# The entry to an FFN: where five transposed tiles are put, who evicts them, and in which order three accumulators are filled

## The chip, the cores and the metric

The kernel runs on one NeuronCore of a Trainium2 chip. The metric is the device time of one execution in microseconds. The kernel before was run three times: 1008.08, 1010.73 and 1012.32 us, median 1010.73.

Names of engines in the profile: PE is TensorE (matmuls and transposes), DVE is VectorE, ACT is ScalarE, POOL is GpSimd, SP is SyncE, which up to now issues all DMAs. PEld is TensorE's loading of weights.

## The reference

The kernel computes one block of a network over a sequence of L = 2048 positions of width D = 640: a layer norm with modulation, an S4D convolution over the sequence, a second layer norm with modulation, and a gated FFN of inner width 1728.

```python
mod = (_silu(c) @ w_mod).reshape(c.shape[0], 6, 1, -1)
sa, ca, ga, sb, cb, gb = ...
h = _layernorm(x) * (1 + ca) + sa
x = x + ga * S4D(h)                       # long convolution by FFT
h = _layernorm(x) * (1 + cb) + sb
gate = h @ w1                             # [2048, 640] @ [640, 1728]
up   = h @ w3
out  = (_silu(gate) * up) @ w2            # [2048, 1728] @ [1728, 640]
x = x + gb * out
```

All in float32. The change touches the second layer norm of the first quarter of the positions and the FFN's first tiles.

## The kernel before, in words

The first 390 us compute the S4D branch: tables, the kernel's spectrum, the transforms, their product, and the first half of the inverse transform, whose result goes to a DRAM tensor `zd`. Their order is laid down by a planner (`Plan`, with ranks written into the file), and all their instructions carry line 156.

What follows is in program order with priorities, and a scheduler of the tile framework orders each engine's instructions from it. The 2048 positions are worked on in four blocks b = 0 to 3 of 512 positions. `self.x2[b]` holds a block as 128 partitions x 4 groups j x 640, and KT = 5 counts the chunks k of 128 channels.

Entry to the FFN, block 0, in this order:

- `inverse_load` (L630) reads the last 128 channels of `zd` for block 0 into the two tiles `izb0` and `izb1`, in four DMAs of 128 KB, all on SP's queue. They wait for the last store to `zd` (`zd<-zt`). Behind them SP issues `load_x2(1)`, four loads of 320 KB into `x2[1]`, then four more for `x2[2]` and eight `iz` loads.
- `inverse` (L640) multiplies them by `wd` into tiles `iy` in PSUM (L647), and DVE adds these to `x2[0]` (L650).
- `ln2` (L661) takes the statistics (L341, L345, a reciprocal square root of 13 small DVE instructions, L320 to L332), normalises the four groups j (`xn`, two on ACT at L674, two on DVE at L672), and transposes `xn` chunk by chunk: for each k four 128x128 transposes into one PSUM bank `tp` (L680). Then DVE makes `v` from the bank (L682, scale and shift), ACT makes `xh`, the same value rounded to float32r, from the same bank (L683), and DVE, or POOL for odd k in block 0, makes the rest `xl = v - xh` (L684). So a float32 product is done as three float32r matmuls: `wh*xh + wh*xl + wl*xh`.
- `ffn` (L728) goes through 14 tiles m of the inner width, in the order 0, 13, 1, 2, ... 12. `up` (L747) fills accumulators `gu`: two (gate and up) for a full tile, one for the half tile 13, which holds both halves. Each takes 15 matmuls (5 chunks x 3; L753, L754, L755). `gate` (L759) makes `th` on ACT (L767), `a` on DVE (L768, L769), `ah` on ACT and `al` on DVE (`split`, L657 to L659); for tile 13 it takes `th` and `u` on ACT (L773, L775) and more on DVE. `down` (L783) multiplies `ah` and `al` by `w2` into the five accumulators `acc` (L788 to L790), one tile behind `up`.
- The weights of the next tiles are split into `wh` and `wl` on ACT (L658) and DVE (L659) as soon as the tile two before has been used up. Those of the first two tiles are ready before the entry.

PSUM has eight banks. In this stage five belong to the pool `po`, one for each `acc`, and three to the tag `gu` of the pool `ps`, shared by the accumulators `gu`, by the tiles `iy` of the inverse transform (its remaining units are worked in between the FFN tiles of block 0), by `tp`, and by the output's transposes `to`. A `gu` bank is free again once its readers are done: for tile 0's first accumulator that is L768, for its second L769, for tile 13's the instruction at L777.

Of the kernel before, what the change touches and what calls it, by code (L numbers as in the profile page):

```python
# [10 lines left out]
F32 = mybir.dt.float32  # L11
F32R = mybir.dt.float32r
I32 = mybir.dt.int32
AF = mybir.ActivationFunctionType
ALU = mybir.AluOpType
# [3 lines left out]
P = 128  # L19
L = 2048  # L20
D = 640
KT = D // P
# [255 lines left out]
class K:  # L278
# [348 lines left out]
            self.nc.sync.dma_start(self.x2[b][q * 32:(q + 1) * 32], self.xv[q, :, 4 * b:4 * b + 4, :])  # L627


    def inverse_load(self, name, pool, tag, bufs, j0, nj, d0, d1):  # L630

        zv = self.zd.rearrange("f r t d -> (f r) t d")
        z = [pool.tile([P, nj, d1 - d0], F32, name=f"{name}{pr}", tag=f"{tag}{pr}", bufs=bufs) for pr in range(2)]
        for pr in range(2):
            for g in range(2):
                t0 = 16 * (2 * pr + g) + j0
                self.zload = self.nc.sync.dma_start(z[pr][g * 64:(g + 1) * 64], zv[:, t0:t0 + nj, d0:d1])
        return z

    def inverse(self, j0, nj, z, ps, tag, bufs, d0, d1):  # L640
# [17 lines left out]
        self.nc.scalar.activation(H, v, AF.Copy)  # L658
        eng.tensor_tensor(Lo, v, H.bitcast(F32), op=ALU.subtract)  # L659

    def ln2(self, b, pool, ps, stats=None, tag="gu"):  # L661

        nc = self.nc
        xs = self.x2[b]
        st, mv = stats or self.ln_begin(pool, f"n{b}")
        for j in range(4):
            self.ln_part(st, xs, j, KT - 1 if stats else 0, KT)
        rstd, nb = self.ln_end(pool, st, mv, f"n{b}")
        xn = pool.tile([P, 4, D], F32, name=f"xn{b}", tag="xn", bufs=1)
        for j in range(4):  # L670
            if j % 2:
                nc.vector.tensor_scalar(xn[:, j, :], xs[:, j, :], rstd[:, j:j + 1], nb[:, j:j + 1], op0=ALU.mult, op1=ALU.add)  # L672
            else:
                nc.scalar.activation(xn[:, j, :], xs[:, j, :], AF.Identity, scale=rstd[:, j:j + 1], bias=nb[:, j:j + 1])  # L674
        xh = pool.tile([P, KT, 512], F32R, name=f"xh{b}", tag="xh", bufs=2)
        xl = pool.tile([P, KT, 512], F32R, name=f"xl{b}", tag="xl", bufs=2)
        for k in range(KT):
            pt = ps.tile([P, 512], F32, name=f"tp{b}{k}", tag=tag, bufs=4 if tag == "f" else 3)
            for j in range(4):
                nc.tensor.transpose(pt[:, j * P:(j + 1) * P], xn[:, j, k * P:(k + 1) * P], self.ident)  # L680
            v = pool.tile([P, 512], F32, name=f"v{b}{k}", tag="v", bufs=2)
            nc.vector.tensor_scalar(v, pt, self.cols[:, 1, k:k + 1], self.cols[:, 0, k:k + 1], op0=ALU.mult, op1=ALU.add)  # L682
            nc.scalar.activation(xh[:, k, :], pt, AF.Identity, scale=self.cols[:, 1, k:k + 1], bias=self.cols[:, 0, k:k + 1])  # L683
            (nc.gpsimd if b == 0 and k % 2 else nc.vector).tensor_tensor(xl[:, k, :], v, xh[:, k, :].bitcast(F32), op=ALU.subtract)  # L684
        return xh, xl

    def weights(self, b, m, wp):
# [40 lines left out]
    def ffn(self, nxt, wp, pool, ps, po, mid):  # L728

        pend = None  # L730
        for b in range(4):
            acc = [po.tile([P, 512], F32, name=f"acc{b}{k}", tag=f"acc{k}") for k in range(KT)]
            for i in range(14):
                m = self.ORDER[i]
                wh, wl, w2h, w2l = self.ahead.pop((b, i), None) or self.weights(b, m, wp)
                gu = self.up(b, m, wh, wl, *nxt[b], ps)
                if pend is not None:
                    self.down(*pend)
                    if i == 0:
                        self.output(b - 1, pend[1], pool, ps)  # L740
                ah, al = self.gate(b, m, gu, pool)
                pend = (m, acc, ah, al, w2h, w2l)
                mid(b, i)
        self.down(*pend)
        self.output(3, acc, pool, ps)

    def up(self, b, m, wh, wl, xh, xl, ps):  # L747
        nc = self.nc
        gu = []
        for i in range(2 if m < 13 else 1):  # L750
            pg = ps.tile([P, 512], F32, name=f"gu{b}_{m}{i}", tag="gu", bufs=3)
            for k in range(KT):
                nc.tensor.matmul(pg, wh[:, i, k, :], xh[:, k, :], start=(k == 0), stop=False)  # L753
                nc.tensor.matmul(pg, wh[:, i, k, :], xl[:, k, :], start=False, stop=False)  # L754
                nc.tensor.matmul(pg, wl[:, i, k, :], xh[:, k, :], start=False, stop=(k == KT - 1))  # L755
            gu.append(pg)
        return gu

    def gate(self, b, m, gu, pool):  # L759
# [53 lines left out]
    def run(self):  # L813
# [7 lines left out]
        def open_(name, side=None, bufs=1, space=None):  # L821
            scopes[name] = ExitStack()
            return self.pool(name, bufs=bufs, space=space, ctx=scopes[name], side=side)
# [19 lines left out]
        nc = self.nc = Engines(self, real)  # L843
# [16 lines left out]
        b = NB - 1  # L860
# [14 lines left out]
        cut = b * P  # L875
        z = {}
# [19 lines left out]
        xp, ip, wp = self.xp, self.ip, self.wp  # L896
        pool = open_("ffn", "right")
        close("psx", "psg")
        po = open_("po", space=PSUM)
        ps = open_("ps", space=PSUM)  # L900
        self.x2 += [pool.tile([P, 4, D], F32, name=f"x2{b}") for b in range(1, 4)]
        z = self.inverse_load("izb", ip, "izb", 1, 0, 4, cut, D)
        self.inverse(0, 4, z, ps, "gu", 3, cut, D)
        nxt = {0: self.ln2(0, pool, ps, self.stats)}
        self.at(2000)
        self.load_x2(1)

# [563 lines left out]
```

## Time and profile before

| | |
|---|---|
| median of 3 runs | 1010.73 us (1008.08 to 1012.32) |
| profiled execution | 1012.95 us, its span 1010.6 us |
| TensorE busy in the span | 891.2 us, 88% |
| VectorE, ScalarE, GpSimd busy | 656.8, 507.8, 279.4 us |
| mean granted TensorE clock | 0.962 |
| first FFN matmul of block 0 | 408.28 us after the span's start |

The span runs from the first to the last instruction; the execution's time holds 2.35 us around it. In the profile a matmul's record lasts longer than its distance to the next one, since matmuls are pipelined: the row says 0.39 us for one of 512 columns, but they follow each other every 0.23 us at full clock and every 0.43 us at half clock. A row of the chain of waits gives start, length, engine and tile, in the order of time; a row of the timeline adds in brackets how long the engine sat idle before it and what ended that.

### The profile page before, as it was taken

What the parts mean: (1) busy time and instruction counts of PE and PEld (TensorE: products, weight loads), DVE (VectorE), ACT (ScalarE), POOL (GpSimd) and SP (SyncE); (2) the same over time, 40 slices, a digit from 0 to 9 for tenths busy, and PEclk for the clock granted to TensorE, in tenths of its full rate; (3) what the DMA queues carried; (4) which work ended last, traced back from release to release, by engine and by line L of the source; (5) the groups of instructions that cost most, each with busy time, mean ns of one, the idle gap of its engine ahead of it and who ended that gap; (6) DMA issues with size and microseconds to landing.
All of it is one profiled execution on the core that took longest, in us unless ns stands there. A gap on an engine that the chain in (4) does not pass through costs nothing.

```text
span 1010.6 us, 20260 instructions
## 1 busy us (share of the span) xinstructions
PE 891.2 (88%) x8129; PEld 714.0 (71%) x8129; DVE 656.8 (65%) x1214; ACT 507.8 (50%) x843; POOL 279.4 (28%) x288
## 2 busy tenths in 40 slices
PE   1463878788999885999999999999999999999996
PEld 1132756767887773677788888888888888888884
DVE  6998999999999475677664453464543643634332
ACT  6878787989787541432243343343433432533231
POOL 1798798988998200100000000000000000000000
PEclk9887998999999897899999999999999999999998
DMA  9955553624131759976232363332534333533302
GB/s 214 266 183 174 120 135 95 152 65 107 44 86 51 192 137 229 232 176 164 86 94 76 107 157 91 94 101 66 138 110 117 83 86 93 146 102 92 103 14 53
DMA packets 140998, 122.05 MB, mean 121 GB/s; under 512 B 13416, under 2 KB 124776, under 8 KB 139368
## 3 DMA queue, kind: packets, MB, share of 16 engines
q1 hardware_dynamic: 140904, 120.75, 45.4%
q8 instruction: 64, 1.05, 0.4%
q14 instruction: 30, 0.25, 0.1%
HBM read 99.75 MB, written 20.97 MB: 119 GB/s over the span
## 4 chain that ended last, share of the span: by engine, by line
PE 73%; DVE 12%; DMA 6%; ACT 3%; issue 3%; SPq 1%; POOL 0%; DVEq 0%; ACTq 0%; POOLq 0%
PE gu L753 12%; PE gu L754 12%; PE gu L755 12%; PE acc L788 6%; PE acc L789 6%; PE acc L790 6%; PE ps L156 4%; DVE yy L156 3%; PE fk L156 3%; PE kps L156 2%; PE fh L156 2%; DMA sp<-in_w_mod 2%; PE fz L156 2%; DVE fp L156 2%; PE iy L647 2%
## 5 line engine op out<-in xcount | busy, mean ns | idle before, releaser
L754 PE MATMUL gu<-xl,wh 128*128 128x512 f32 x540 | 212.6, 394 | 0.0
L753 PE MATMUL gu<-xh,wh 128*128 128x512 f32 x540 | 212.0, 393 | 0.5 <-ACT xh L683 0.5
L755 PE MATMUL gu<-xh,wl 128*128 128x512 f32 x540 | 211.7, 392 | 0.0
L658 ACT ACTIVATE wh<-wr 128x640 fp32r<-128x640 f32 x105 | 72.0, 732 | 136.3 <-PE gu L754 136.3
L721 POOL MEMSET w2l<- 64x640 f32 x3 | 1.9, 628 | 451.0 <-PE acc L789 451.0
L753 PEld LDWEIGHTS gu<-xh,wh 128*128 128x128 f32 x540 | 101.8, 188 | 25.6 <-issue 1.0
L754 PEld LDWEIGHTS gu<-xl,wh 128*128 128x128 f32 x540 | 101.9, 189 | 21.8
L755 PEld LDWEIGHTS gu<-xh,wl 128*128 128x128 f32 x540 | 101.8, 188 | 21.8
L788 PE MATMUL acc<-ah,w2h 128*128 128x512 f32 x260 | 103.8, 399 | 0.0
L789 PE MATMUL acc<-ah,w2l 128*128 128x512 f32 x260 | 102.2, 393 | 0.0
L768 DVE SCALAR_TENSOR_TENSOR a<-th,gu 128x512 f32<-128x512 f32 x52 | 35.8, 688 | 99.2 <-ACT th L767 99.0
L767 ACT ACTIVATE th<-gu 128x512 f32<-128x512 f32 x52 | 31.1, 598 | 135.4 <-PE gu L755 135.4
L769 DVE TENSOR_TENSOR a<-a,gu 128x512 f32<-128x512 f32 x52 | 35.7, 687 | 97.3 <-PE gu L755 97.2
L790 PE MATMUL acc<-al,w2h 128*128 128x512 f32 x260 | 96.5, 391 | 0.0
L156 POOL TENSOR_TENSOR yy<-e,e 128x512 f32<-128x512 f32 x80 | 86.3, 1095 | 16.6 <-PE kps L156 11.7
L659 DVE TENSOR_TENSOR wl<-wr,wh 128x640 fp32r<-128x640 f32 x105 | 82.2, 819 | 10.6 <-ACT wh L658 10.6
L156 POOL TENSOR_TENSOR ph<-p,p 128x1024 int32<-128x1024 int32 x40 | 79.0, 1975 | 7.3 <-ACT tr L156 6.6
L156 PE MATMUL kps<-yy,xx 128*32 128x64 f32 x2560 | 51.3, 234 | 31.3 <-DVE xx L156 23.4
L658 ACT ACTIVATE w2h<-w2r 128x640 fp32r<-128x640 f32 x51 | 37.6, 737 | 81.5 <-issue 42.6
L659 DVE TENSOR_TENSOR w2l<-w2r,w2h 128x640 fp32r<-128x640 f32 x51 | 42.0, 823 | 56.2 <-ACT w2h L658 56.0
L156 DVE TENSOR_TENSOR yy<-yy,tr 128x512 f32<-128x512 f32 (+1 forms) x80 | 75.5, 946 | 0.9 <-ACT tr L156 0.6
L156 PEld LDWEIGHTS kps<-yy,xx 128*32 128x32 f32 x2560 | 44.7, 116 | 41.2 <-issue 25.0
(204 smaller groups left out, 1646.6 us busy)
## 6 DMA issues: line engine op xcount, KB each, us to landing
wr<-in_w SPq DMA_DIRECT2D x104, 320.0 KB, 3.9
w2r<-in_w SPq DMA_DIRECT2D x52, 320.0 KB, 3.0
zd<-zt SPq DMA_DIRECT2D x40, 256.0 KB, 3.2
iz<-zd SPq DMA_DIRECT2D x24, 320.0 KB, 5.8
xs<-in_x SPq DMA_DIRECT2D x16, 320.0 KB, 11.4
hs<-hb SPq DMA_DIRECT2D x20, 256.0 KB, 2.4
xb<-hs SPq DMA_DIRECT2D x20, 256.0 KB, 4.8
x<-in_x SPq DMA_DIRECT2D x16, 320.0 KB, 11.0
```

Source lines behind the costliest of these rows:

```text
L156: self.prev = self.k.order(f(*a, **kw), self.prev)
L658: self.nc.scalar.activation(H, v, AF.Copy)
L659: eng.tensor_tensor(Lo, v, H.bitcast(F32), op=ALU.subtract)
L753: nc.tensor.matmul(pg, wh[:, i, k, :], xh[:, k, :], start=(k == 0), stop=False)
L754: nc.tensor.matmul(pg, wh[:, i, k, :], xl[:, k, :], start=False, stop=False)
L755: nc.tensor.matmul(pg, wl[:, i, k, :], xh[:, k, :], start=False, stop=(k == KT - 1))
L767: nc.scalar.activation(th, gu[0], AF.Tanh, scale=0.5)
L768: nc.vector.scalar_tensor_tensor(a, th, 1.0, gu[0], op0=ALU.add, op1=ALU.mult)
L769: nc.vector.tensor_mul(a, a, gu[1])
L788: nc.tensor.matmul(acc[k], w2h[:, sl], ah, start=(m == 0), stop=False)
L789: nc.tensor.matmul(acc[k], w2l[:, sl], ah, start=False, stop=False)
L790: nc.tensor.matmul(acc[k], w2h[:, sl], al, start=False, stop=(m == 12))
```

## The change

Four parts, all at the entry to the FFN of block 0, with some of `ln2` changed for every block:

1. `inverse_load` takes a second engine: of each pair of `izb` loads the second is issued by ACT instead of SP.
2. In block 0 the five `tp` tiles go to the five banks of `po` that become `acc` later, instead of through the three `gu` banks. `ffn` therefore takes the `acc` tiles only when the first `down` is about to be placed.
3. A `tp` bank is read once: `v` is made from it, by DVE for even k and by ACT for odd k in block 0 (by DVE in the other blocks). `xh` is then a copy of `v` out of SBUF on ACT, and `xl` comes from POOL for odd k in block 0. `v` has three buffers instead of two.
4. `up` can take several tiles. For block 0 the tiles 0 and 13 are worked together: for each chunk k the nine matmuls of all three accumulators, then the next k. For all other tiles the order stays: one accumulator after the other.

In the built program TensorE then has the 20 transposes in a row (the first two of each tile, then the last two of each), the 45 matmuls, three `iy` tiles, ten `down` matmuls, an `iy` tile, five `down` matmuls, and the next tile. ACT has, after `xh` and a table load: `th` of tile 0, two `wh`, two more `wh`, `th` and `u` of tile 13, `ah` of tile 0. Before, `ah` stood between the first two and the second two `wh`.

```diff
-    def inverse_load(self, name, pool, tag, bufs, j0, nj, d0, d1):
+    def inverse_load(self, name, pool, tag, bufs, j0, nj, d0, d1, other=None):
...
-                self.zload = self.nc.sync.dma_start(z[pr][g * 64:(g + 1) * 64], zv[:, t0:t0 + nj, d0:d1])
+                (other if g and other else self.nc.sync).dma_start(z[pr][g * 64:(g + 1) * 64], zv[:, t0:t0 + nj, d0:d1])
...
-            pt = ps.tile([P, 512], F32, name=f"tp{b}{k}", tag=tag, bufs=4 if tag == "f" else 3)
+            if po:
+                pt = po.tile([P, 512], F32, name=f"tp{b}{k}", tag=f"acc{k}")
+            else:
+                pt = ps.tile([P, 512], F32, name=f"tp{b}{k}", tag="gu", bufs=3)
...
-            v = pool.tile([P, 512], F32, name=f"v{b}{k}", tag="v", bufs=2)
-            nc.vector.tensor_scalar(v, pt, self.cols[:, 1, k:k + 1], self.cols[:, 0, k:k + 1], op0=ALU.mult, op1=ALU.add)
-            nc.scalar.activation(xh[:, k, :], pt, AF.Identity, scale=self.cols[:, 1, k:k + 1], bias=self.cols[:, 0, k:k + 1])
-            (nc.gpsimd if b == 0 and k % 2 else nc.vector).tensor_tensor(xl[:, k, :], v, xh[:, k, :].bitcast(F32), op=ALU.subtract)
+            v = pool.tile([P, 512], F32, name=f"v{b}{k}", tag="v", bufs=3)
+            if po and k % 2:
+                nc.scalar.activation(v, pt, AF.Identity, scale=self.cols[:, 1, k:k + 1], bias=self.cols[:, 0, k:k + 1])
+            else:
+                nc.vector.tensor_scalar(v, pt, self.cols[:, 1, k:k + 1], self.cols[:, 0, k:k + 1], op0=ALU.mult, op1=ALU.add)
+            self.split(xh[:, k, :], xl[:, k, :], v, nc.gpsimd if po and k % 2 else nc.vector)
...
-            acc = [po.tile([P, 512], F32, name=f"acc{b}{k}", tag=f"acc{k}") for k in range(KT)]
+            acc = None
             for i in range(14):
                 m = self.ORDER[i]
-                wh, wl, w2h, w2l = self.ahead.pop((b, i), None) or self.weights(b, m, wp)
-                gu = self.up(b, m, wh, wl, *nxt[b], ps)
+                if b == 0 and i < 2:
+                    if i == 0:
+                        w = [self.ahead.pop((0, x)) for x in range(2)]
+                        both = self.up(0, [(self.ORDER[x], *w[x][:2]) for x in range(2)], *nxt[0], ps)
+                    w2h, w2l = w[i][2:]
+                    gu = both[i]
+                else:
+                    wh, wl, w2h, w2l = self.ahead.pop((b, i), None) or self.weights(b, m, wp)
+                    gu, = self.up(b, [(m, wh, wl)], *nxt[b], ps)
...
+        gu = [[ps.tile([P, 512], F32, name=f"gu{b}_{m}{i}", tag="gu", bufs=3) for i in range(2 if m < 13 else 1)] for m, _, _ in tiles]
+        every = [(pg, wh[:, i], wl[:, i]) for (m, wh, wl), g in zip(tiles, gu) for i, pg in enumerate(g)]
+        for ks in [(k,) for k in range(KT)] if len(tiles) > 1 else [range(KT)]:
+            for pg, wh, wl in every:
+                for k in ks:
+                    nc.tensor.matmul(pg, wh[:, k, :], xh[:, k, :], start=(k == 0), stop=False)
+                    nc.tensor.matmul(pg, wh[:, k, :], xl[:, k, :], start=False, stop=False)
+                    nc.tensor.matmul(pg, wl[:, k, :], xh[:, k, :], start=False, stop=(k == KT - 1))
...
-        z = self.inverse_load("izb", ip, "izb", 1, 0, 4, cut, D)
+        z = self.inverse_load("izb", ip, "izb", 1, 0, 4, cut, D, nc.scalar)
         self.inverse(0, 4, z, ps, "gu", 3, cut, D)
-        nxt = {0: self.ln2(0, pool, ps, self.stats)}
+        nxt = {0: self.ln2(0, pool, ps, self.stats, po)}
```

More of the change, by code (lines that the diff above doesn't have):

```diff
@@ L659, in split, with ln2 @@
         eng.tensor_tensor(Lo, v, H.bitcast(F32), op=ALU.subtract)
-    def ln2(self, b, pool, ps, stats=None, tag="gu"):
+    def ln2(self, b, pool, ps, stats=None, po=None):
         nc = self.nc
@@ L740, in ffn @@
                         self.output(b - 1, pend[1], pool, ps)
+                if acc is None:
+                    acc = [po.tile([P, 512], F32, name=f"acc{b}{k}", tag=f"acc{k}") for k in range(KT)]
                 ah, al = self.gate(b, m, gu, pool)
@@ L745, in ffn, with up @@
         self.output(3, acc, pool, ps)
-    def up(self, b, m, wh, wl, xh, xl, ps):
+    def up(self, b, tiles, xh, xl, ps):
         nc = self.nc
[L749 to L756, printed above, removed]
+        gu = [[ps.tile([P, 512], F32, name=f"gu{b}_{m}{i}", tag="gu", bufs=3) for i in range(2 if m < 13 else 1)] for m, _, _ in tiles]
[6 more added lines that the diff above has]
+                    nc.tensor.matmul(pg, wl[:, k, :], xh[:, k, :], start=False, stop=(k == KT - 1))
         return gu
```

## The prediction

> **What bounds the kernel now.** I read the page's summary first, then the chain of waits, then busy time by stretches.
>
> ```profile
> span 1010.6 us, 20260 instructions
> ...
> PE   1463878788999885999999999999999999999996
> ```
>
> ```profile
> core 0: us, PE busy (x) PEld busy (x) DVE busy (x) ACT busy (x) POOL busy (x), PEclk, DMA share, GB/s
> 402.00:420.40 18.40, 16.92 (x67) 13.59 (x69) 9.50 (x14) 8.71 (x13) 2.54 (x2) 0.74 1.02 237
> 420.40:460.00 39.60, 39.60 (x186) 28.56 (x187) 29.46 (x83) 12.88 (x20) 0.00 (x0) 1.00 0.82 193
> ```
>
> ```profile
> PE to L804 <- ACT oc L801: 0.5, 2, 0.3
> ```
>
> The last fence is the whole answer to what TensorE waited for between 420 and 1010 us: 0.5 us. From the second row on it is busy 39.60 of 39.60 us. So the FFN is bound by TensorE from its first block to the end, and a gain in the entry to it shifts everything behind it by the same amount, no more. The change can win only in the thin slices around 386 to 420 us, and every new TensorE wait behind that is lost in full. The chain of waits through the entry:
>
> ```profile
> 391.30 3.53 DMA izb<-zd
> ...
> 394.97 1.53 PE iy L647 x7
> ...
> 402.14 1.98 PE tp L680 x8
> ...
> 408.28 0.79 PE gu L753
> ...
> 420.37 1.23 PE iy L647 x8
> ...
> 426.47 0.43 PE gu L753
> ```
>
> Four stations count: the last of the four `izb` loads frees TensorE at 394.97; transposes start at 402.14; the first FFN matmul starts at 408.28; the first 45 of them (tiles 0 and 13) are done at 420.37, and the next tile begins at 426.47, after one `down` (15 matmuls) and four `iy` tiles, without a gap. I carry these stations through the change.
>
> **1. Two of the four `izb` loads move to ACT's queue.**
>
> ```profile
> 389.35 2.56 SPq L637 DMA_DIRECT2D izb<-zd  x4
> 391.95 4.05 SPq L627 DMA_DIRECT2D x<-in_x  x8
> ```
>
> ```profile
> 393.05 1.51 PE L647 MATMUL iy<-izb,wd 128*64 128x128 f32 x6 [6.17 <-DMA izb<-zd]
> ```
>
> ```profile
> ACT xn L674 <- DVE rs_n_n L332: 14.1, 1, 14.1
> ```
>
> SP needs 2.56 / 4 = 0.64 us for each issue. With two issuers the last load starts after one issue instead of three: 1.3 us earlier. TensorE needs the first two loads, works 1.51 us on them, then needs the others. The second load would start 0.64 us earlier, so TensorE begins at 393.05 - 0.64 = 392.41 and is ready for the others at 393.92, while these land at 394.83 - 1.28 = 393.55. It goes on at 393.92 instead of 394.97: **-1.05 us**, I take -1.0. On ACT the two issues cost nothing: it idles 14.1 us there, waiting for the row statistics. No DMA from ACT is in this trace. Its price is bounded by -1.3 (issue time alone counts) and by a loss, which is the rival C below. Moving two issues off SP also starts the eight `x` loads behind them 1.3 us earlier.
>
> **2. Five transposed tiles at once, and one eviction each.**
>
> ```profile
> 402.14 2.82 PE L680 MATMUL tp<-ident,xn 128*128 128x128 f32 x12 [5.23 <-ACT xn L674]
> ```
>
> ```profile
> L680 PE MATMUL tp<-ident,xn 128*128 128x128 f32 x20 | 4.8, 427 | 6.1 <-ACT xn L674 5.2 <-ACT xh L683 0.9
> ...
> L682 DVE TENSOR_SCALAR v<-tp,cols 128x512 f32<-128x512 f32 x5 | 4.0, 809 | 2.6 <-PE tp L680 1.8 <-POOL xl L684 0.5
> L683 ACT ACTIVATE xh<-tp,cols 128x512 fp32r<-128x512 f32 x5 | 3.8, 778 | 4.3 <-DVE v L682 4.3
> ...
> L684 POOL TENSOR_TENSOR xl<-v,xh 128x512 fp32r<-128x512 f32 x2 | 2.5, 1270 | 58.0 <-DMA x<-in_x 56.3 <-ACT xh L683 1.7
> L684 DVE TENSOR_TENSOR xl<-v,xh 128x512 fp32r<-128x512 f32 x3 | 2.1, 689 | 1.0 <-ACT xh L683 0.8
> ```
>
> In the built program the first halves of all five tiles go ahead of the second halves of any, so tile 0 is complete after 12 transposes instead of 8. One costs (2.82 - 0.42) / 11 = 0.22 us, so the first eviction starts 0.87 us later: a loss. From there (times as if part 1 had not been): DVE's `v0` 405.02 to 405.84; ACT evicts tile 1 from 405.46 to 406.25, and then makes `xh0` out of `v0` in SBUF, 0.63 us by the `ah` row below, to 406.88. TensorE starts the three accumulators at 406.93 instead of 408.28: before, it had to make two more tiles first, whose banks were held by two evictions in series. **-1.35 us.** Does it starve then? Each k brings nine matmuls of 0.23, 2.1 us. `xl0` (DVE, 0.69) is there at 407.6, as the first three matmuls end; `xl1` (POOL, 1.27, after `xh1` at 407.5) at 408.85, needed at 409.7; the last tile's chain `xl2`, `v4`, `xh4`, `xl4` ends near 411.1, needed at 415.2. So no wait, and DVE, ACT and POOL stay hidden.
>
> **3. The clock.** 45 matmuls at 0.2287 us are 10.3 us; before, they took 420.37 - 408.28 = 12.09, since the first ran at half clock. On a grid of 3.41 us the granted clock changes at the ends:
>
> ```profile
> 206.78:210.20 3.42, 1.82 (x25) 1.00 0.14 39
> 210.20:213.61 3.41, 1.87 (x68) 1.00 0.02 5
> ...
> 374.03:377.45 3.42, 1.21 (x10) 1.00 0.95 231
> 377.45:380.86 3.41, 3.41 (x31) 0.50 1.13 272
> ...
> 401.34:404.75 3.41, 2.61 (x12) 0.50 1.00 218
> ...
> 408.17:411.58 3.41, 3.30 (x8) 0.50 1.03 251
> 411.58:414.99 3.41, 3.41 (x17) 1.00 1.03 243
> ```
>
> (Columns: stretch, length, TensorE busy, clock, DMA.) A window 76% busy (2.61) left it at half; one at 97% (3.30) raised it. After the change the 20 transposes (4.4 us) run without a break and the matmuls follow 0.4 us later, so the first window that begins after 402.14 is the full one, and it ends between 405.55 and 408.97 depending on where the grid lies in that run. Half clock costs the matmuls 0 to 1.0 us then, 0.2 at the middle; I take 0.3 instead of 1.8: **-1.5 us** (0 if the 0.4 us gap spoils the window, -1.8 at best). T, the end of the 45 matmuls, thus moves from 420.37 to 406.93 + 10.3 + 0.3 - 1.0 = 416.5: **-3.85 us**.
>
> **4. What comes late next: the gate.** Before, tile 0's accumulators were done some 4 us ahead of tile 13's, and its gate ran under tile 13's matmuls. Now all three finish within the last 1.37 us, and all three `gu` banks are held, so the `iy` tiles and `down` stand behind the gate. Rows of the gate:
>
> ```profile
> 416.52 0.60 ACT L767 ACTIVATE th<-gu 128x512 f32<-128x512 f32 x1 [4.14 <-PE gu L755]
> 417.01 1.36 ACT L658 ACTIVATE wh<-wr 128x640 fp32r<-128x640 f32 x2
> ...
> 417.15 0.69 DVE L768 SCALAR_TENSOR_TENSOR a<-th,gu 128x512 f32<-128x512 f32 x1 [5.35 <-ACT th L767]
> 417.77 0.83 DVE L659 TENSOR_TENSOR wl<-wr,wh 128x640 fp32r<-128x640 f32 x1
> ...
> 418.52 0.68 DVE L769 TENSOR_TENSOR a<-a,gu 128x512 f32<-128x512 f32 x1
> ...
> 419.23 0.63 ACT L658 ACTIVATE ah<-a 128x512 fp32r<-128x512 f32 x1 [0.87 <-DVE a L769]
> ...
> 421.13 0.49 DVE L650 TENSOR_TENSOR x<-iy,x 128x320 f32<-128x320 f32 x1 [0.54 <-PE iy L647]
> ...
> 421.57 0.59 ACT L773 ACTIVATE th<-gu 64x512 f32<-64x512 f32 x1
> 422.06 0.58 ACT L775 ACTIVATE u<-gu 64x512 f32<-64x512 f32 x1
> ```
>
> Counted from T, with these durations and the start-to-start steps between them. ACT: `th` -1.33, two `wh` from -0.84, then in its new order two more `wh` (0.45 to 1.8), tile 13's `th` and `u` (to 2.9), and only then `ah`, 2.85 to 3.5: `ah` now stands behind four instructions that followed it. DVE: `a` ends at 0.0 and frees the first bank, the product ends at 1.35 and frees the second, the `x` add ends at 2.55 and frees the first again. TensorE, 0.62 us a tile (1.23 / 2): `iy` at 0.05, 1.4 and 2.6, then it waits for `ah`; ten `down` matmuls 3.5 to 6.0, the fourth `iy` to 6.6, five more with `al` (ready at 6.1) to 7.95. The next tile starts at T + 7.9, against T + 6.1 before: **+1.8 us**. Bounds: 0 if ACT and DVE hide it, +3.5 if all of the wait for `ah` is added. Behind it TensorE has 3.4 us of `gu` matmuls for each step of the gate, as before, so I see no second gap.
>
> **5. Rest.** In blocks 1 to 3 `xh` is made from `v` (0.63) instead of from the bank (0.78), and the third `v` buffer lets DVE run ahead; TensorE waits 0.5 us in that whole part, so 0. The `acc` banks are taken later but needed later too: 0.
>
> **Sum**: -1.0 - 1.35 - 1.5 + 1.8 = -2.05 us. The profiled execution took 1012.95 us with a span of 1010.6, which gives 1010.9 after; the median of the runs shown is 1010.73, 2.2 below that execution, so the forecast for the median is **1008.7 us**, -0.2%.
>
> **Rivals.**
>
> A, the gate's gap is hidden or smaller and loads and clock fall well: -1.3 - 1.35 - 1.8 and +0.5 give -4 us, 1006.7. Against it: the new order of ACT is fixed in the program.
>
> B, the clock is lost in the gap. Between T and T + 3.5 TensorE works 1.85 us, 53%. The rows show a window of 53% (1.82) that was followed by full clock and one of 35% (1.21) after which it fell, so this lies just on the safe side. If it falls, one window of 3.41 us runs at half: +1.7, total -0.3, 1010.4. The Trainium skill ("TensorE: Matmul & The Clock Gate", section "HAM oscillation — how this bites in real kernels") warns only of idle gaps above some 3.4 us; by that the gap, broken by three `iy` tiles, is harmless and the sum stays 1008.7. The row of the 35% window disagrees: its longest idle stretch was 2.46 us.
>
> ```profile
> 376.24 1.08 PE L156 MATMUL iy<-iz,wd 128*64 128x512 f32 x4 [2.46 <-DVE x L156]
> ```
>
> C, slower: ACT's loads fall behind the `x` loads.
>
> ```profile
> DMA packets 12112, 14.63 MB, mean 225 GB/s; under 512 B 779, under 2 KB 10123, under 8 KB 11723
> ```
>
> (The transfers between 375 and 440 us.) On one queue the `izb` loads were ahead of the `x` loads. On two they share the engines with the first four `x` loads (1.31 MB, 5.8 us at that 225 GB/s), which SP now issues 1.3 us earlier. If ACT issues late, its last load meets them: held up by half of them it lands at 393.55 + 2.9 = 396.45, by all at 399.3. Without its gain the change stands at -1.05, so it is even with a landing at 394.83 + 1.05 = 395.9 and slower behind that: +0.6 for half, +3.4 for all, 1012.8 in the middle. Against it: both issuers wait for the same store and would start together, and then the `izb` packets of both queues are through before the first `x` packet. For it: a load of 0.64 us of issue on an engine that had no DMA in this trace. The Trainium skill ("DMA: Bandwidth & Descriptors", section "Issuing engines are not separate DMA queues") says that transfers started by different engines run on the same 16 DMA engines and interleave, and that a second issuer saves only issue time. By that rule the four `x` loads are a rival whenever they overlap, and the time is nearer 1012.8 than 1008.7; no run yet shows two queues.
>
> **Numbers.** Forecast as summed 0.62, A 0.12, B 0.11, C 0.15. The range reaches from A with the spread of the runs (1008.08 to 1012.32, about 2 us either way) to C: 1005.2 to 1013.6. Half a percent is 5.05 us and about what a measurement of this kernel tells from no change; no case alone passes it, only A or C together with that spread: faster 0.10, same 0.80, slower 0.10.
>
> **What would show it.** `izb` waits ending near 394 instead of 394.97; 20 transposes in one run; the first `gu` matmul some 4.8 us after the first transpose instead of 6.1; full clock within about 1 us of it; TensorE waits of 0.3 to 0.8 us on DVE and ACT right behind the 45 matmuls, `down` waiting for `ah`; then no waits. Wrong would make me: `izb` landing after 395.9, a clock of 0.5 behind T, or a TensorE wait in a later tile.

## The result and the profile after

The changed kernel took 1015.93 us (median of 7 runs, 1012.67 to 1017.53), the kernel before in the same series 1012.44 us. The ratio is 1.0035, 95% interval 1.0019 to 1.0051: a loss of about 3.5 us, or 0.35%, where 0.2% of gain was forecast; the median lies above the forecast range, which ended at 1013.6, and the kernel before itself had a median 1.7 us higher in this series of seven than in its first three runs. The profiled execution took 1017.53 us, with a span of 1015.7.

The chain of waits through the entry, after the change (start, length, what; all in us):

```profile
389.63 2.28 DMA zd<-zt
391.94 0.65 ACTq L637
392.63 8.41 DMA izb<-zd
401.17 1.53 PE iy L647 x7
...
408.34 3.26 PE tp L683 x14
...
412.97 0.97 PE gu L769 x3
...
427.16 0.51 PE acc L803
...
431.79 0.23 PE gu L769
```

The last store to `zd` landed 2.6 us later than in the profiled execution before. That lies ahead of everything the change touches, so I count all stations from the first `izb` issue, which follows that landing at once: 389.35 before, 391.93 after (both on SP). The third row is the loss: a load of 128 KB, issued by ACT, that took 8.41 us to land, at 401.04. The stations then read:

| us | before | after | difference | forecast |
|---|---|---|---|---|
| first `izb` issue to the start of the transposes | 12.79 | 16.41 | +3.62 | -1.0 |
| transposes to the first `gu` matmul | 6.14 | 4.63 | -1.51 | -1.35 |
| 45 `gu` matmuls | 12.09 | 10.63 | -1.46 | -1.5 |
| their end to the next tile | 6.10 | 8.10 | +2.0 | +1.8 |
| first transpose to the end of the span | 608.46 | 607.36 | -1.10 | -1.05 |

The last row is the sum of the three above it and of all that follows; it is read from the span (1010.6 - 402.14 and 1015.7 - 408.34). Of the four steps three came out within 0.2 us, and one had the wrong sign.

TensorE by stretches in the kernel before, then in the changed one (columns: stretch, length, busy time and number of instructions of PE, PEld, DVE, ACT, POOL, then the granted clock, DMA share, GB/s):

```profile
402.14:408.28 6.14, 4.79 (x21) 3.99 (x21) 3.54 (x6) 3.03 (x4) 1.27 (x1) 0.50 0.97 221
408.28:420.37 12.09, 12.09 (x47) 9.56 (x49) 5.79 (x9) 5.51 (x8) 1.27 (x1) 0.86 1.04 245
```

```profile
408.34:412.97 4.63, 4.04 (x20) 3.80 (x20) 1.77 (x4) 2.10 (x4) 0.00 (x0) 0.63 1.02 238
412.97:423.60 10.63, 10.62 (x45) 8.29 (x45) 4.30 (x6) 5.55 (x9) 2.57 (x2) 1.00 1.02 232
423.60:431.70 8.10, 6.89 (x32) 3.78 (x33) 7.98 (x17) 3.46 (x6) 0.00 (x0) 1.00 0.61 168
```

The clock rises within the 20 transposes now (0.63 on average, 0.50 before), and the 45 matmuls run at full clock without a gap. Behind them the clock stays at 1.00.

What TensorE waited for from 388 to 402 us, and from 404 us on, after the change:

```profile
PE iy L647 <- DMA izb<-zd: 10.0, 2, 5.7
...
PE tp L683 <- ACT xn L674: 5.2, 1, 5.2
PE gu L769 <- ACT xh L658: 0.6, 1, 0.6
PE iy L647 <- DVE a L784: 0.5, 1, 0.5
PE to L819 <- ACT oc L816: 0.5, 2, 0.3
PE iy L647 <- DVE x L650: 0.4, 1, 0.4
PE acc L803 <- ACT ah L658: 0.3, 1, 0.3
```

Three small waits stand behind the 45 matmuls, as forecast (0.5, 0.4 and 0.3 us). Later there is only the 0.5 us before `to`, which the kernel before has too. So the loss is in the first row.

### The profile page after: what moved, and what is told of

It is laid out like the page before. It is cut to its first block, busy times and chain, and to the rows that moved or that the text cites. A ratio compares the mean times of both kernels' runs of the same rounds, so it can differ in the third digit from the quotient of the medians.

```text
span 1015.7 us, 20252 instructions
## 1 busy us (share of the span) xinstructions
PE 892.4 (88%) x8129; PEld 713.3 (70%) x8129; DVE 655.7 (65%) x1212; ACT 506.8 (50%) x845; POOL 279.5 (28%) x288
## 3 DMA queue, kind: packets, MB, share of 16 engines
q8 instruction: 64, 1.05, 0.4%
## 4 chain that ended last, share of the span: by engine, by line
PE 73%; DVE 14%; ACT 4%; issue 3%; DMA 3%; POOL 1%; SPq 1%; ACTq 0%; DVEq 0%
PE gu L770 12%; PE gu L771 12%; PE gu L769 12%; PE acc L803 6%; PE acc L804 6%; PE acc L805 6%; PE ps L156 4%; PE kps L156 3%; DVE yy L156 3%; PE fz L156 3%; PE fk L156 2%; PE fh L156 2%; DVE fp L156 2%; DVE xx L156 2%; DVE hn L156 2%
## 5 line engine op out<-in xcount | busy, mean ns | idle before, releaser
L659 DVE TENSOR_TENSOR wl<-wr,wh 128x640 fp32r<-128x640 f32 x105 | 82.1, 819 | 10.6 <-ACT wh L658 10.6
```

## The experiments

Two explanations of the late load were open. **X**: SP's `x` loads, which now run beside ACT's `izb` loads on another queue, hold these up. **Q**: a load issued by ACT is slow by itself. A third, **S**, was that the late `zd` store was part of the loss. Each experiment gives a ratio to the kernel before, with its 95% interval; two kernels were run once, and have a profile but no ratio. "Start of the transposes" is counted from the first `izb` issue of the same profile.

**One queue again.**

```diff
-        z = self.inverse_load("izb", ip, "izb", 1, 0, 4, cut, D, nc.scalar)
+        z = self.inverse_load("izb", ip, "izb", 1, 0, 4, cut, D)
```

> All four izb loads on SP again, the rest as changed. In the changed kernel TensorE goes on after the last izb load 9.25 us behind the landing of the last zd store (before: 5.64), the transposes and the 45 matmuls gain 1.5 us each, the gate loses 2.0. My theory (ACT's load is held up by the x loads): TensorE goes on at 5.6 us again, the other three stay, so 3.6 us faster than the changed kernel and 1.0 us faster than before, a ratio to before of 0.999. Rival S (the loss is no matter of the queues: the last zd store itself landed 2.6 us later in the profiled execution, because of the change): the zd store stays late, and the kernel stays 1.5 us slower than before, ratio 1.0015. Rival Q (ACT's queue is slow by itself) expects the same as my theory here.

Ratio 0.9988 (0.9973 to 1.0004). SP's queue and the transposes:

```profile
392.52 2.57 SPq L637 DMA_DIRECT2D izb<-zd  x4
```

```profile
405.04 4.21 PE L683 MATMUL tp<-ident,xn 128*128 128x128 f32 x20 [5.23 <-ACT xn L674]
```

The transposes start at 12.52; from there to the end it is 607.36 us, exactly the changed kernel's. So the loss goes with the second queue. S falls too: the last `zd` store landed even later in this profile (first `izb` issue at 392.52, 391.93 in the changed kernel), and the loss is gone all the same. Over all fourteen profiles that issue lies between 387.6 and 392.5. The rest of the change is worth about 1.1 us, which agrees with the ratio, though the interval just includes no change.

**The second queue alone, in the kernel before.**

```diff
-                self.zload = self.nc.sync.dma_start(z[pr][g * 64:(g + 1) * 64], zv[:, t0:t0 + nj, d0:d1])
+                (other if g and other else self.nc.sync).dma_start(z[pr][g * 64:(g + 1) * 64], zv[:, t0:t0 + nj, d0:d1])
...
-        z = self.inverse_load("izb", ip, "izb", 1, 0, 4, cut, D)
+        z = self.inverse_load("izb", ip, "izb", 1, 0, 4, cut, D, nc.scalar)
```

> The kernel before, with two of the four izb loads on ACT and nothing else changed. My theory and rival Q: TensorE goes on 9.2 us behind the last zd store instead of 5.64, nothing behind it makes that good, so 3.6 us slower than before: ratio 1.0036. Rival S: no loss from the loads, ratio 0.999 to 1.000.

Ratio 1.0024 (1.0012 to 1.0035). The load that ACT issued second:

```profile
388.34 7.61 DMA izb<-zd
```

The transposes start at 15.61, 2.8 us later than before, and 608.55 us remain from there. The loss stands alone, a little smaller than in the changed kernel. X and Q are still both possible.

**The `x` loads held, first version, and two of them let through.**

```diff
-    def load_x2(self, b):
+    def load_x2(self, b, behind=None):
         for q in range(4):
+            if behind is not None:
+                self.nc.gpsimd.tensor_copy(self.x2[b][q * 32:(q + 1) * 32, 0, :1], behind[q * 32:(q + 1) * 32])
             self.nc.sync.dma_start(self.x2[b][q * 32:(q + 1) * 32], self.xv[q, :, 4 * b:4 * b + 4, :])
...
-        self.load_x2(1)
+        self.load_x2(1, z[1][:, 0, :1])
```

> The changed kernel, two queues, but each x load of block 1 waits on SP for a GpSimd copy of one column of the second izb tile, so that no x load is under way before the izb loads have landed. My theory: the last izb load lands 4.5 to 5 us behind the last zd store (1.0 ahead of before, the gain of step 1), so 4.4 us faster than the changed kernel and 1.5 to 2 us faster than before, ratio 0.998 to 0.9985. Rival Q (ACT's queue is slow by itself): it lands at 9.2 as in the changed kernel, ratio 1.0035 or worse. The x loads come some 5 us later; they are needed only behind the first FFN tiles.

> As the run before, but the first two x loads are let through at once and only the other two (and all behind them on SP) are held: 0.66 MB may run beside the izb loads, 2.9 us at 225 GB/s, instead of up to 2.6 MB. My theory: the last izb load is late by at most these 2.9 us, so it lands 6 to 7.6 us behind the last zd store. Rival Q: 9.2. A third possibility, that any x load on the other queue costs the full 8.4 us: 9.2 too.

Ratio 1.0015 (1.0002 to 1.0028) for the first, with transposes at 15.97; the second, run once (hold only for q >= 2), had them at 16.10. Both seem to speak for Q, and neither does: the hold was not what it was meant to be. On SP the scheduler placed loads of block 2, which nothing held, ahead of the held ones (two in the first kernel, one in the second), and for q = 0 and 1 the copied rows belong to SP's half of the tile, so these went out when SP's load had landed. SP's queue in the first kernel:

```profile
389.44 1.24 SPq L637 DMA_DIRECT2D izb<-zd  x2
390.74 9.34 SPq L629 DMA_DIRECT2D x<-in_x  x8
```

The `x` loads began 1.30 us behind the first `izb` load, as without a hold. What the second kernel does show is that three `x` loads beside the `izb` loads are enough for nearly the whole delay: SP issued three from 390.10 on and the next at 398.01, and the last `izb` load landed 8.8 us behind the first issue (9.1 in the changed kernel). My bound of 2.9 us for two of them was not tested.

**Everything on SP held.**

```diff
     def load_x2(self, b):
+        b and self.nc.gpsimd.tensor_copy(self.x2[b][:, 0, :1], self.zb[:, 0, :1])
         for q in range(4):
...
         for pr in range(2):
+            name in ("iz2", "iz3") and self.nc.gpsimd.tensor_copy(z[pr][:, 0, :1], self.zb[:, 0, :1])
             for g in range(2):
...
-        z = self.inverse_load("izb", ip, "izb", 1, 0, 4, cut, D, nc.scalar)
+        z = _, self.zb = self.inverse_load("izb", ip, "izb", 1, 0, 4, cut, D, nc.scalar)
```

> The hold of the x loads done again, since in the first version the scheduler put four loads of block 2 ahead of the held ones. Now every x load and the iz loads of the next two units wait for a GpSimd copy of a column of the second izb tile, so SP sends nothing between its two izb loads and the landing of the last one. My theory (ACT's load is held up by the x loads): the last izb load lands 4.5 to 5 us behind the last zd store, the kernel is about 1.8 us faster than before, ratio 0.998. Rival Q (ACT's queue is slow by itself): it lands at 8.5 or later with nothing beside it, ratio 1.001 or worse.

Ratio 0.9978 (0.9965 to 0.9992). SP's queue, and TensorE on the `izb` tiles, with everything held:

```profile
390.02 1.25 SPq L637 DMA_DIRECT2D izb<-zd  x2
395.01 2.41 SPq L628 DMA_DIRECT2D x<-in_x  x3
```

```profile
393.42 3.15 PE L647 MATMUL iy<-izb,wd 128*64 128x128 f32 x16 [5.75 <-DMA izb<-zd]
```

With nothing else under way TensorE no longer waits between the two pairs of loads: its 16 matmuls run in one go. The transposes start at 11.78, that is 1.01 us earlier than in the profile before, as much as step 1 had forecast. ACT's queue is not slow by itself, Q falls, and X stands. The packets of the two queues in the same stage say it directly. The first pair of rows is the kernel with everything held, 390 to 394.5 us, the second the changed kernel, 395 to 400.4 us (queue: packets, MB, share of the 16 engines; q1 is SP's, q10 ACT's; the row below gives a load's size in KB and its median time to landing in us):

```profile
q10 hardware_dynamic: 544, 0.26, 22.5%
q1 hardware_dynamic: 544, 0.26, 22.2%
...
izb<-zd ACTq DMA_DIRECT2D x2, 128.0 KB, 3.8
```

```profile
DMA packets 425, 1.30 MB, mean 241 GB/s; under 512 B 71, under 2 KB 310, under 8 KB 310
...
q1 hardware_dynamic: 200, 1.19, 94.0%
q10 hardware_dynamic: 225, 0.11, 8.8%
```

Held, both queues finish their 544 packets, and ACT's loads land in 3.8 us. In the changed kernel 225 packets of ACT's queue, 0.11 MB, took more than five microseconds. Beside them went 200 packets of SP's queue, which carried ten times the bytes: 115 of them (425 less the 310 under 8 KB) were `x` pieces of 10240 bytes.

**The same `x` loads in pieces of 2560 bytes instead of 10240.**

```diff
-        self.x2 += [pool.tile([P, 4, D], F32, name=f"x2{b}") for b in range(1, 4)]
+        self.x2 += [pool.tile([P, 4, D + 4], F32, name=f"x2{b}")[:, :, :D] for b in range(1, 4)]
```

> The changed kernel with four unused floats behind each row of the x2 tiles of blocks 1 to 3, so that an x load moves pieces of 2560 bytes instead of 10240; the bytes and the issues are the same. My theory in its finer form (the two queues take turns piece by piece, so a 512-byte piece waits for the piece ahead of it): the delay shrinks to about a quarter, the last izb load lands 5.5 to 7 us behind the last zd store. Rival B (the queues share by bytes) and rival Q: 8.5 to 9.3 as in the changed kernel.

Run once: the last `izb` load landed 7.8 us behind the first issue, against 9.1 in the changed kernel, and the transposes started at 15.10. With pieces of 10240 bytes the kernel with the second queue alone had the landing at 8.3, so the delay shrank by 0.5 to 1.3 us, by one profile; it did not shrink to a quarter. The two queues from 393 to 397 us:

```profile
DMA packets 592, 0.90 MB, mean 226 GB/s; under 512 B 48, under 2 KB 287, under 8 KB 592
...
q1 hardware_dynamic: 371, 0.80, 85.3%
q10 hardware_dynamic: 221, 0.11, 12.9%
```

Per packet of ACT's queue 1.4 `x` pieces went through (592 - 287 = 305 to 221) instead of 0.5 (115 to 225), so with smaller pieces more of them go through, though in bytes fewer. Neither "piece by piece" nor "equal bytes" describes that; the rule of sharing stays open. The Trainium skill ("DMA: Bandwidth & Descriptors", section "Queues, rings and completion order") says that each DMA engine takes turns between the queues, and changes only at the end of a packet of several descriptors. The turns agree with these rows; how many descriptors a turn holds can't be read from them.

**The gap behind the 45 matmuls: `ah` on VectorE, and `up` tile by tile.** The first makes `ah` of tile 0 without waiting for ACT, the second undoes part 4 of the change (`ffn` and `up` as before). Both keep the `izb` loads on one queue.

```diff
-    def split(self, H, Lo, v, eng):
-        self.nc.scalar.activation(H, v, AF.Copy)
+    def split(self, H, Lo, v, eng, first=None):
+        first.tensor_copy(H, v) if first else self.nc.scalar.activation(H, v, AF.Copy)
...
-            self.split(ah, al, a, nc.vector)
+            self.split(ah, al, a, nc.vector, nc.vector if b == m == 0 else None)
```

> One queue for the izb loads, and ah of the first tile of block 0 is made by VectorE right behind the product instead of by ScalarE behind four other instructions. In the trace with one queue the first down matmul starts 3.9 us after the last of the 45 gu matmuls started its successor's place. Expected: down starts about 1.4 us earlier, and the kernel is 1.2 us faster than with one queue alone, ratio to before 0.9975. Rival: VectorE, which also makes the x additions that free the gu banks, gets late by the 0.6 us of the copy, the iy tiles wait instead, and the time is that of one queue alone, 0.9988.

Ratio 0.9985 (0.9974 to 0.9997), and 607.68 us from the transposes to the end: no gain over one queue alone (0.9988, 607.36). In this profile the 45 matmuls took 11.01 us at a mean clock of 0.96, where nine other kernels with the five banks took 10.64 to 10.66; that is the difference of 0.3 us. VectorE's part:

```profile
416.31 0.69 DVE L783 SCALAR_TENSOR_TENSOR a<-th,gu 128x512 f32<-128x512 f32 x1 [5.51 <-ACT th L782]
416.94 0.83 DVE L659 TENSOR_TENSOR wl<-wr,wh 128x640 fp32r<-128x640 f32 x1
417.68 0.68 DVE L784 TENSOR_TENSOR a<-a,gu 128x512 f32<-128x512 f32 x1
418.28 0.82 DVE L659 TENSOR_TENSOR wl<-wr,wh 128x640 fp32r<-128x640 f32 x1
419.01 0.48 DVE L650 TENSOR_TENSOR x<-iy,x 128x320 f32<-128x320 f32 x1
419.41 0.82 DVE L659 TENSOR_TENSOR wl<-wr,wh 128x640 fp32r<-128x640 f32 x1
420.15 0.42 DVE L658 CAST ah<-a 128x512 fp32r<-128x512 f32 x1
```

Between each two steps of the gate stands a `wl` of 0.82 us, the split of the next tiles' weights. So `ah` comes as late from VectorE as it did from ACT (done 3.5 us behind the last of the 45 matmuls in both kernels), and the product and the `x` additions, which free the `gu` banks, come no earlier.

> One queue, and part 4 of the change undone: up takes one tile at a time again and acc is taken at the start of the block, as before. My theory: the gap behind the 45 matmuls does not come from part 4 but from the transposes leaving the three gu banks free (part 2): all three accumulators are then open at once and the scheduler fills them side by side anyway, so the time is that of one queue alone, ratio to before 0.9988. Rival (part 4 makes the gap): tile 0 is complete 3.4 us ahead of tile 13 again, its gate runs under tile 13's matmuls, and the kernel is 2 us faster than one queue alone, 0.997.

Ratio 0.9992 (0.9977 to 1.0006), 607.38 us from the transposes to the end, and the same three waits behind the 45 matmuls: part 4 does nothing. The first FFN matmuls:

```profile
405.65 0.97 PE L758 MATMUL gu<-xh,wh 128*128 128x512 f32 x3 [0.48 <-ACT xh L658]
```

Three of one source line in a row are three accumulators begun side by side; in the kernel before, L753, L754 and L755 followed each other in turn. Once the transposes sit in the `acc` banks (part 2) all three `gu` banks are free, and the scheduler fills them side by side whether the code says so or not. So the gate's gap needs no part 4. I put it down to part 2; part 3, which this kernel has too, was not run apart.

**One queue, everything held.** The hold as above, without `nc.scalar`.

> The same hold of the x and iz loads, but all four izb loads on SP: it parts the gain of the second queue from that of the hold. My theory: the second queue itself saves issue time, so with one queue TensorE goes on 5.3 to 5.6 us behind the last zd store and the transposes start 12.3 to 12.8 us behind it (with the hold and two queues 11.8), ratio to before 0.9985 to 0.999. Rival (the hold earns it all, since the x loads slow the izb loads on one queue too): transposes at 11.8, ratio 0.998.

Ratio 0.9971 (0.9956 to 0.9986); transposes at 12.22. Five profiles with one queue and no hold have them at 12.28, 12.52, 12.61, 12.79 and 13.81 (mean 12.80); three with two queues and the hold at 11.64, 11.78 and 11.90. By the stations the second queue earns 0.4 us beyond the hold, with only one profile of a held kernel on one queue; by the times the two held kernels (0.9971 and 0.9978) can't be told apart. Whether the hold helps on one queue stays open as well: 12.22 is hardly below the 12.28 of a kernel without it, and the intervals of 0.9971 and 0.9988 overlap.

**`wl` of the next two tiles on GpSimd**, with `ah` on VectorE and one queue; then the same with two queues and the hold; then that with `ah` on ACT.

```diff
-                self.split(wh[:, i], wl[:, i], raw[:, i], self.nc.vector)
+                self.split(wh[:, i], wl[:, i], raw[:, i], self.nc.gpsimd if b == 0 and m in (1, 2) else self.nc.vector)
```

> One queue, ah of the first tile on VectorE, and the four wl of the tiles 1 and 2 of block 0 made by GpSimd, which is idle there, instead of VectorE. In the run with ah alone VectorE had the four wl of 0.82 us each between a, the product, the x addition and ah, and that held the iy tiles and down. My theory (VectorE's queue makes the gap, not ScalarE's): the product, the x additions and ah come 0.7 to 2 us earlier, the gap behind the 45 matmuls shrinks by 1.2 to 1.5 us, ratio to before 0.9975. Rival: GpSimd takes some 1.6 us for each wl, the next tile's come too late and TensorE waits there: no gain or a loss, 0.9988 or more.

> All together: two queues with the hold, ah on VectorE, wl of the tiles 1 and 2 on GpSimd. If the gains add: 0.9978 for the held loads and 0.0013 for the gap, ratio to before 0.9965, some 3.5 us faster than before. If the wl come too late: 0.998 or more.

> As the run before, with ah on ScalarE as in the change. The scheduler then puts all four iy tiles and the first accumulator of the next tile ahead of down, so that down no longer waits for ah. Theory: the same 0.9965, since the iy tiles wait for VectorE's product and x additions and these come early. Rival: ah was what counted, 0.9975 or more.

On one queue: 0.9978 (0.9962 to 0.9994), 606.76 us from the transposes to the end, 0.6 less than with one queue alone, where 1.2 to 1.5 were expected. TensorE's waits behind the 45 matmuls shrink to one of 0.4 us. Two queues, hold and both edits: 0.9968 (0.9950 to 0.9985), median 1008.58 us, which by the two ratios beats the kernel before by about 3 us and the changed one by about 7; it can't be told apart from the two held kernels without its other edits. The last kernel is no gain, 1.0008 (0.9992 to 1.0024). TensorE's longest wait behind its entry, and ACT at that place:

```profile
PE acc L803 <- ACT ah L658: 3.1, 1, 3.1
```

```profile
435.36 0.74 ACT L658 ACTIVATE wh<-wr 128x640 fp32r<-128x640 f32 x1 [5.21 <-DMA wr<-in_w]
436.00 0.61 ACT L658 ACTIVATE ah<-a 128x512 fp32r<-128x512 f32 x1
```

`ah` of tile 1 stands on ACT behind a `wh` that waits 5.21 us for its weights. On SP's queue one of the next four weight loads went out at 418.92, then four `iz` loads, and the other three weight loads only from 423.45 on; in the kernel with both edits three weight loads stood ahead of the `iz` loads, and in the one with the hold alone all four. The other three held kernels have no such wait. So the loss goes with the order that the scheduler chose on SP's queue for this edit; whether the hold has a part in it was not shown.

## Why the prediction was wrong

- **Step 1, the loads, failed, in size and sign:** -1.0 forecast, +3.6 measured. What I left out of the sum was that the order on one queue protected the `izb` loads. The argument against rival C was that all `izb` packets would be through before the first `x` packet. My own numbers denied it: the `x` loads were to be issued 1.3 us earlier, at 390.65, and the last `izb` load was to land at 393.55, 2.9 us behind that. The argument holds for 1.3 us of issue, not for 2.9 us of transfer.
- **The 1.0 us of step 1** is there without SP's other loads (11.78 against 12.79), but by another split: TensorE began 3.40 us behind the first issue instead of 3.70, which is 0.30 earlier where 0.64 was forecast, and then ran through both pairs of loads without a break. It did the same once on one queue without the hold (the kernel tile by tile, transposes at 12.28), and the held kernel with one queue (12.22) leaves only 0.4 to the second issuer. That the total met the forecast is in part luck.
- **Rival C, at 0.15, is what happened in effect,** though not by its condition: it supposed that ACT issues late, and ACT's first issue came at 391.94, beside SP's at 391.93. Counted from the same issue as before the landing would be 389.35 + 9.11 = 398.5, between C's half (396.45) and its whole (399.3). Its time of 1012.8 against 1010.73 is a loss of 2.1 us; the stations give 3.6 - 1.1 = 2.5, the ratio 3.5 (1.9 to 5.2). The rule of the Trainium skill that I cited ("DMA: Bandwidth & Descriptors", section "Issuing engines are not separate DMA queues") spoke for C, and the traces agree with it: 8.41 us for the load beside the `x` loads, 3.8 without them.
- **Step 2, the transposes, was right:** -1.51 measured for -1.35.
- **Step 3, the clock, was right:** 10.63 us for the 45 matmuls, none at half clock, against 10.6. The 0.3 us set aside for half clock was not needed; the 45 took that much longer than 45 times 0.2287 us, so the exact agreement is luck. The step itself is not: counted to the first `iy` matmul behind it the stretch took 10.66 us here, 10.64 to 10.66 in nine more kernels with the five banks, and 10.98 and 11.01 in the other two.
- **Step 4, the gate, was right in size and half right in cause:** T + 8.1 for T + 7.9. I named ACT's order as what makes `ah` late, and `ah` did start 2.85 us behind the matmuls, as the list has it. But with `ah` taken off ACT nothing was gained, so VectorE's `wl` between the steps count as much. That the gap comes without part 4 I had not seen.
- **Step 5, nothing later, was right:** no new wait behind the entry, and 607.36 us from the transposes on.
- **Rival A** did not come, **rival B** neither: the clock stayed at 1.00 in the 8.1 us behind the matmuls, 6.89 of them busy. In their first 3.5 us TensorE was busy for 2.35, 67% where B had reckoned with 53%, so B's case was not tried.

So the forecast of a small gain fell by one term of four, the one for which the trace had no row.

## What to carry to other kernels

A queue is also an order. Before moving a load to another engine's queue, look at what follows it on the old one: if large transfers stand behind it, they no longer wait, and a small urgent load shares the DMA engines with them. Where a scheduler fills idle engines by readiness, freeing a resource (here three PSUM banks) can change the order of the work more than rewriting the loop does: here the loop could be put back and nothing changed.

## What the runs showed of the hardware

**Two queues on the same DMA engines.** With 10240-byte pieces on SP's queue, 225 packets of ACT's queue went through beside 115 such pieces in 5.4 us of the changed kernel, so that ACT's 0.11 MB took as long as SP's 1.19 MB; a load that takes 3.8 us with nothing beside it took 8.41. Four times smaller pieces gave back only 0.5 to 1.3 us.

**GpSimd slows VectorE.** While GpSimd made `wl` (all four in 7.20 us), a VectorE copy and a subtraction with all their operands in SBUF took over twice as long. GpSimd and VectorE in the kernel with all edits:

```profile
418.26 7.20 POOL L659 TENSOR_TENSOR wl<-wr,wh 128x640 fp32r<-128x640 f32 x4 [6.88 <-ACT wh L658]
```

```profile
419.10 1.00 DVE L658 CAST ah<-a 128x512 fp32r<-128x512 f32 x1
420.02 0.48 DVE L650 TENSOR_TENSOR x<-iy,x 128x320 f32<-128x320 f32 x1
420.43 1.64 DVE L659 TENSOR_TENSOR al<-a,ah 128x512 fp32r<-128x512 f32 x1
```

The copy to `ah` took 0.42 us without it and 1.00 with it, `al` 0.68 and 1.64 (on one queue 1.00 and 1.65); the `x` addition, which reads one operand from PSUM, took 0.48 in both. Not everything in SBUF was slowed alike: `u`, a product on 64 partitions, went from 0.69 to 0.95, and the statistics (`st_n`), with a single input, kept their 0.28. Part of the gain expected from GpSimd may have gone there. The Trainium skill ("SBUF — State Buffer", section "SBUF: two separate sides") says that VectorE and GpSimd share a pair of ports that one of them holds for a whole instruction, and the waits fit that: the copy ended 0.3 us and `al` 0.6 us behind the end of a `wl`.
